# One tile turned by TensorE, sign bits folded into ten weight chunks, three engines' shares moved, and a new written order

## The chip, the cores and the metric

The kernel runs on one core of one Trainium2 chip. The metric is the time of one execution on the device, in microseconds (us); the time before is a median of 3 runs. TensorE does the matmuls (PE in the profile, PEld its weight loads), VectorE (DVE), ScalarE (ACT) and GpSimd (POOL) work beside it, and SyncE (SP) issues nearly all transfers (DMA).

## What is computed

Three layers follow each other, all results in float32: linear attention over 8 batches of 576 tokens with 8 heads of 64, a dense layer with a softmax-weighted activation and a layer norm, and a mixture of 8 experts of which each token takes one.

```python
# attention, per batch and head
q_s = softmax(q, axis=-1);  k_s = softmax(k, axis=2)
x = q_s @ (k_s.T @ v)                      # -> 4608 tokens x 512
# dense layer: w_in 512x1024, w_out 1024x512, both float64 in memory
h = x @ w_in
solu = h * softmax(h)
x2 = (layernorm(solu) * g_ln) @ w_out
# experts: w1 8x512x1024, w2 8x1024x512
logits = x2 @ w_gate + modality_bias[modality_id];  e = argmax(logits)
out = gate * (relu(x2 @ w1[e]) @ w2[e])
```

## The kernel before

A number that is multiplied is held as two float16 halves, `hi` and `lo`, and a product is three matmuls. So every operand passes a pair of steps: `hi_part` (ScalarE, a copy with a scale) and `lo_part` (the difference, on VectorE or GpSimd). Scales are powers of two, found from a maximum over all partitions: `diagonals` writes 128x128 diagonal matrices, a matmul with ones spreads them, and VectorE reduces.

The head of the program prepares weights. `w_in` and `w_out` come as float64 in 8 chunks of 128x512 each, and `to_f32` makes float32 of each by integer work. ScalarE makes the scaled high word (`p`, in PSUM), GpSimd makes 13 low bits (`x`), and VectorE joins them in two passes (the low bits, L618, then the sign, L620). One chunk of sixteen, number 14, is *folded*: its sign bits are put beside its low bits first, and VectorE needs one pass (L615). Chunks 0 to 7 are w_in, 8 to 15 are w_out in the order of rows `WO`.

Then the tokens pass in 36 tiles of 128. For tile t: `xT_mm` makes attention's output, `h_mm` (two halves of 12 matmuls) multiplies by w_in, `ln_unit` makes exp, norm and the halves `zhl` (ScalarE `za`, then VectorE `zl`, L1022), a DMA transpose turns `zhl` into `lnT` (`tr`, L1026), and `x2_mm` (48 matmuls, L1087) multiplies by w_out. `kv_mm` comes once a batch (60 matmuls, L869). `w_col` (96 small matmuls, L719) multiplies the turned w_out (`w_out_tr`, DMA transposes, L686) by the gate's weights once, and `w_col_split` puts the result beside w_out, so the first `x2_mm` needs it. After the tiles come 18 slots of 256 routed tokens (`slot_mm`, L1531 and L1552), each with 4 MB of expert weights, and a short tail.

Each step is a generator: `at(time, step)` files it, and every `yield` starts its next part. The string `ORDER` names all parts, some 2,900, in the order in which they are written into the program: an engine's own instructions run in that order, and an engine that waits holds up what is written behind it on the same engine. SP's transfers are in the same order. Tiles of PSUM named `big` (`ph`, `px`, `pcv`) share three buffers.

Of the kernel before, what the change touches and what calls it, by code (L numbers as in the profile page):

```python
# [73 lines left out]
w_col:7#0.0 zl:#0.0 ex:#10.0 w_col:6#0.0 v_split:1,3#0.1 tr:#35.0 w_col:3#0.0 v_split:1,1#0.0 v_split:1,2#0.1
w_col:5#0.0 ex:#10.1 v_split:1,4#0.1 ex:#39.0 w_col:2#0.0 lo:#10.0 mx:#12.0 w_col:4#0.0 zz:#1.1 tt:#2.0 h_mm:3,1#0.0
mx:#38.1 k_load:2,0#0.0 ex:#42.0 tr:#10.0 v_split:1,0#0.1 w_col_split:#0.0 ex:#40.0 fc:#0.1 ex:#38.0 w_col_split:#0.1
v_split:1,1#0.1 sq:#2.0 x2_mm:0#0.0 zl:#1.0 fc:#0.2 tr:#37.0 mx:#12.1 sc:#2.0 ex:#12.0 fc:#0.3 su:#4.0 zz:#2.0
su:#6.0 v_load:2#0.0 ex:#12.1 mx:#41.0 zz:#2.1 su:#4.1 kv_mm:1#0.0 mx:#11.0 ex:#41.0 zl:#2.0 fs:#0.0 hi:#36.0 hi:#4.0
tt:#3.0 tr:#39.0 lo:#36.0 kv_evac:1#0.0 sq:#3.0 x2_mm:1#0.0 lo:#12.0 tr:#38.0 sc:#3.0 kv_evac:1#0.1 su:#6.1 su:#5.0
v_sum:2,0#0.0 q_load:7#0.0 hi:#6.0 k_load:2,3#0.0 lo:#68.0 su:#5.1 zz:#3.0 kv_evac:1#0.2 hi:#5.0 v_sum:2,3#0.0  # L80
lo:#37.0 mx:#44.0 v_sum:2,4#0.0 xT_mm:4#0.0 lo:#38.0 tr:#40.0 x2_mm:2#0.0 xT_evac:4#0.0 mx:#44.1 hi:#37.0
q_load:9#0.0 v_sum:2,1#0.0 q_load:8#0.0 lo:#69.0 mx:#11.1 zz:#3.1 route:#0.0 xT_evac:4#0.1 route:#0.1 ex:#11.0
zl:#3.0 ex:#44.0 fc:#1.0 fc:#1.1 route:#0.2 mx:#14.0 su:#7.0 route:#0.3 h_mm:4,0#0.0 route:#0.4 v_sum:2,2#0.0
# [1776 lines left out]
```

## Time and profile before

| | us |
|---|---|
| median of 3 runs (lowest to highest) | 930.58 (930.48 to 931.44) |
| the profiled execution, own time | 932.11 |
| its span, from first to last record | 930.4 |
| PE busy (share of the span) | 847.3 (91%) |
| DVE busy | 776.5 (83%) |
| ACT busy | 700.5 (75%) |
| POOL busy | 520.4 (56%) |

The profiled execution lasted 1.5 us longer than the median, and 1.7 us of it lie outside the span. A busy PE is not a PE at its peak: a matmul's record covers its way through the array. PE's clock is full nearly everywhere; the granted clock falls below it at 50 to 60 us and 80 to 100 us, in one stretch at 380 to 400 us, and at the end.

### The profile page before, as it was taken

What the parts mean: (1) busy time and instruction counts of PE and PEld (TensorE: products, weight loads), DVE (VectorE), ACT (ScalarE), POOL (GpSimd) and SP (SyncE); (2) the same over time, 40 slices, a digit from 0 to 9 for tenths busy, and PEclk for the clock granted to TensorE, in tenths of its full rate; (3) what the DMA queues carried; (4) which work ended last, traced back from release to release, by engine and by line L of the source; (5) the groups of instructions that cost most, each with busy time, mean ns of one, the idle gap of its engine ahead of it and who ended that gap; (6) DMA issues with size and microseconds to landing.
All of it is one profiled execution on the core that took longest, in us unless ns stands there. A gap on an engine that the chain in (4) does not pass through costs nothing.

```text
span 930.4 us, 18754 instructions
## 1 busy us (share of the span) xinstructions
PE 847.3 (91%) x6565; PEld 585.7 (63%) x6565; DVE 776.5 (83%) x1589; ACT 700.5 (75%) x1041; POOL 520.4 (56%) x886
## 2 busy tenths in 40 slices
PE   0387999999998989898999999999999999999992
PEld 0264866686675766667667766756666666666671
DVE  6999789988987878788988699998889888888850
ACT  5658687977785887675687498877888888887851
POOL 7553787887888786754456765132234444434410
PEclk9988999999999999999999999999999999999997
DMA  8989899798699877678778988899999899999910
GB/s 322 293 177 231 179 191 207 163 225 186 134 203 194 175 166 153 159 102 212 176 185 230 277 259 241 263 279 320 303 301 275 273 286 286 270 288 272 273 66 12
DMA packets 275770, 204.83 MB, mean 220 GB/s; under 512 B 217617, under 2 KB 220241, under 8 KB 275666
## 3 DMA queue, kind: packets, MB, share of 16 engines
q1 hardware_dynamic: 268226, 183.51, 77.8%
q0 software_dynamic: 7152, 20.01, 6.4%
q8 instruction: 53, 0.87, 0.4%
q14 instruction: 51, 0.42, 0.1%
q10 hardware_dynamic: 288, 0.02, 0.0%
HBM read 130.94 MB, written 19.86 MB: 162 GB/s over the span
## 4 chain that ended last, share of the span: by engine, by line
PE 27%; DVE 27%; issue 12%; POOL 11%; ACT 10%; DMA 8%; SPq 2%; POOLq 0%; ACTq 0%; DVEq 0%
PE spo L1552 9%; PE sph L1531 8%; PE px L1087 6%; PE ph L968 3%; DVE t L998 3%; DVE hmx L986 2%; DMA out_dram<-kt,six 2%; DVE zhl L1022 2%; DMA six<-perm_scr 2%; DVE w1b L499 2%; ACT w1b L492 2%; DVE vhl L499 1%; POOL out_dram L1480 1%; ACT w2b L492 1%; DVE smm L1378 1%
## 5 line engine op out<-in xcount | busy, mean ns | idle before, releaser
L1087 PE MATMUL px<-w2b,lnT 128*128 128x256 f16 x1728 | 198.8, 276 | 4.0 <-DMA lnT<-zhl 4.0
L968 PE MATMUL ph<-w1b,xTt 128*128 128x512 f16 x864 | 198.3, 383 | 3.5 <-DVE rlg L1109 2.6
L1531 PE MATMUL sph<-vhl,w1b 128*128 128x256 f16 x1728 | 192.2, 273 | 1.9 <-DMA vhl<-kTt 1.7
L1552 PE MATMUL spo<-w2b,hh 128*128 128x512 f16 x864 | 191.1, 379 | 2.2 <-DVE hh L1544 2.2
L1087 PEld LDWEIGHTS <-lnT 128*128 128x128 f16 x1728 | 168.9, 98 | 32.5 <-DMA lnT<-zhl 5.8
L1531 PEld LDWEIGHTS <-w1b 128*128 128x128 f16 x1728 | 168.8, 98 | 26.7 <-DMA vhl<-kTt 2.5
L1466 POOL DMA_INDIRECT kTt<-xs_scr,six x38 | 53.7, 1413 | 173.5 <-DMA six<-perm_scr 127.5
L1552 PEld LDWEIGHTS <-hh 128*128 128x128 f16 x864 | 83.8, 98 | 100.9 <-DVE hh L1544 4.5
L968 PEld LDWEIGHTS <-xTt 128*128 128x128 f16 x864 | 82.9, 99 | 95.4 <-issue 6.1
L1480 POOL DMA_INDIRECT out_dram<-kt,six x37 | 48.0, 1298 | 51.3 <-ACT kt L1564 35.2
L992 ACT ACTIVATE e<-ph,hnm,ghb 128x1024 f32<-128x1024 f32 x32 | 38.3, 1197 | 27.7 <-DVE hnm L988 21.0
L1564 ACT ACTIVATE kt<-spo,srs 128x512 f32<-128x512 f32 x36 | 23.1, 682 | 47.8 <-issue 43.1
L499 DVE SCALAR_TENSOR_TENSOR w1b<-raw,sc,w1b 128x1024 f16<-128x1024 f32 x40 | 49.5, 1278 | 10.5 <-ACT w1b L492 10.4
L1016 ACT ACTIVATE e<-t,hna,ha 128x1024 f32<-128x1024 f32 x36 | 44.5, 1236 | 17.1 <-DVE hna L1013 11.9
L900 POOL TENSOR_TENSOR qr<-qr,qmx 128x512 f32<-128x512 f32 x36 | 40.3, 1121 | 23.9 <-DVE hmb L1007 14.4
L1022 DVE TENSOR_TENSOR zhl<-e,zhl 128x1024 f16<-128x1024 f32 x36 | 47.2, 1312 | 6.8 <-ACT zhl L1019 6.6
L1003 ACT ACTIVATE e<-t,hts 128x1024 f32<-128x1024 f32 x36 | 41.2, 1144 | 12.8 <-DVE t L998 11.8
L499 DVE SCALAR_TENSOR_TENSOR w2b<-raw,sc,w2b 128x1024 f16<-128x1024 f32 x40 | 49.9, 1275 | 0.9 <-ACT w2b L492 0.9
L1165 POOL DMA_INDIRECT perm_scr<-ids,rposi x36 | 39.9, 1109 | 16.0 <-POOL rposi L1163 6.5
L1378 DVE TENSOR_REDUCE smm<-raw 128x1 f32<-128x1024 f32 x40 | 47.7, 1208 | 1.0 <-DMA raw<-in_moe_w_dram 1.0
L921 POOL TENSOR_TENSOR qhl<-qr,qhl 128x512 f16<-128x512 f32 x36 | 42.6, 1187 | 10.5 <-ACT qhl L917 10.1
L869 PE MATMUL pk<-vhl,kTt 128*128 128x128 f16 x480 | 31.7, 230 | 16.0 <-DVE vhl L499 9.3
(284 smaller groups left out, 1732.7 us busy)
## 6 DMA issues: line engine op xcount, KB each, us to landing
raw<-in_moe_w_dram SPq DMA_DIRECT2D x88, 512.0 KB
qr<-in_q_dram SPq DMA_DIRECT2D x36, 256.0 KB
...
```

Of the source, the lines that this page charges most:

```text
L499: return e.scalar_tensor_tensor(out=lo, in0=src, scalar=scale, in1=hi, op0=ALU.mult, op1=ALU.subtract)
L921: G.tensor_tensor(out=g["hl"][:, 1], in0=qf, in1=g["hl"][:, 0], op=ALU.subtract)
L968: x = T.matmul(ph[:, n, :], xt[:, a, c, :], w1s[:, b2, c, n * 512:(n + 1) * 512], start=(c == 0 and (a, b2) == (0, 0)), stop=(c == 3 and a ...
L1003: mark["qa", t] = A.activation(out=g["e"], in_=g["t"], func=AF.Square, bias=g["mean"], scale=-1024.0, accum_out=var)
L1016: A.activation(out=g["e"], in_=g["t"], func=AF.Identity, bias=g["na"], scale=g["a"])
L1022: mark["zv", t] = V.tensor_tensor(out=g["z"][:, 1], in0=g["e"], in1=g["z"][:, 0], op=ALU.subtract)
L1087: T.matmul(px[:, n, 0:c1 - c0], lt[:, a, f, :], w2s[:, b2, f, c0:c1], start=(f == 0 and (a, b2) == (0, 0)), stop=(f == 7 and a == 1))
L1378: V.tensor_reduce(out=g["mm"][:, c:c + 1], in_=raws(i, 1, c), axis=AX.X, op=ALU.max, apply_absolute_value=True)
L1466: G.indirect_dma_start(out=gr[h], out_offset=None, in_=xs, in_offset=bass.IndirectOffsetOnAxis(ap=ix[:, h:h + 1], axis=0))
L1480: x = G.indirect_dma_start(out=out, out_offset=bass.IndirectOffsetOnAxis(ap=ix, axis=0), in_=ob, in_offset=None, bounds_check=NTOK - 1, oo ...
L1531: T.matmul(ph[:, ff, :], s1[:, a, c, f * 128:(f + 1) * 128], xt[:, 4 * b2 + c, :], start=(n == 0), stop=(n == 11))
L1552: T.matmul(po[:, h, :], hh[:, a, f, h * 128:(h + 1) * 128], s2[:, b2, f, 0:DM], start=(f == 0 and (a, b2) == (0, 0)), stop=(f == 7 and a = ...
```

## The change

Six things change.

1. Ten chunks are folded instead of one (`FOLD`): 0, 4, 6, 7 of w_in, 8, 9, 10, 13, 14, 15 of w_out. The sign is now a float16 zero with its sign bit, which ScalarE makes from the high word or GpSimd from its upper 16 bits.
2. `either` looks into a list of parts, `ON_POOL`. A part in it goes to another engine than by default. For the sign and the low bits the default is GpSimd and the other is ScalarE (six signs, five low parts). For the diagonals the default is VectorE and the other is ScalarE (five steps, six matrices: w_in, w_out, w_gate with two, v of batches 0 and 1). For three subtractions (`kv_evac` of batch 0, `w_out_split` 0 and 6) the other is GpSimd.
3. Tile 0 (`NTURN = 1`) has no DMA transpose: `turn` multiplies eight blocks of 128x128 of each half by an identity `eyeh` into a `big` tile, and ScalarE copies it to `lnT`.
4. `to_f32` has one more `yield`, so sign, low bits and joining can be placed apart.
5. The table of biases is made later (its two loads stood third and fourth on SP).
6. `ORDER` is written anew throughout.

```diff
-FOLD = (14,)
+FOLD = (0, 4, 6, 7, 8, 9, 10, 13, 14, 15)
+ON_POOL = """
+kv_evac:0#0.2 turn:0#0.1 turn:1#0.1 v_scale:0#0.1 v_scale:1#0.1 w_gate_split:#0.1 w_in_chunk:0,0#0.1
...
+    def either(e=G):
+        return e if here[0] in POOLED else V
...
         for i in range(n):
-            x = V.tensor_scalar(out=dg[:, i, :], in0=eye, scalar1=t[:, i:i + 1], scalar2=None, op0=ALU.mult)
-        return dg[:, 0:n, :], x
+            if either(A) is A:
+                A.activation(out=dg[:, i, :], in_=eye, func=AF.Copy, scale=t[:, i:i + 1])
+            else:
+                V.tensor_scalar(out=dg[:, i, :], in0=eye, scalar1=t[:, i:i + 1], scalar2=None, op0=ALU.mult)
+        return dg[:, 0:n, :]
...
-        G.tensor_scalar(out=xh[:, :, 0] if fold else x, in0=half[:, :, 1], scalar1=2.0 ** -13, scalar2=2.0 ** -14 - 0.5, op0=ALU.mult,
-                        op1=ALU.add)
         if fold:
-            G.tensor_scalar(out=xh[:, :, 1].bitcast(BF16), in0=hi.bitcast(F32), scalar1=0.0, scalar2=None, op0=ALU.mult)
-            yield
+            sign = xh[:, :, 1].bitcast(F16)
+            if either(A) is A:
+                A.activation(out=sign, in_=hi.bitcast(F32), func=AF.Copy, scale=2.0 ** -112)
+            else:
+                G.tensor_scalar(out=sign, in0=half[:, :, 3], scalar1=-2.0 ** -60, scalar2=32767.5 * 2.0 ** -60,
+                                op0=ALU.mult, op1=ALU.add)
+        yield
+        low = xh[:, :, 0] if fold else x
+        if either(A) is A:
+            A.activation(out=low, in_=half[:, :, 1], func=AF.Copy, scale=2.0 ** -13, bias=2.0 ** -14 - 0.5)
+        else:
+            G.tensor_scalar(out=low, in0=half[:, :, 1], scalar1=2.0 ** -13, scalar2=2.0 ** -14 - 0.5, op0=ALU.mult,
+                            op1=ALU.add)
+        yield
...
-        mark["kvv", b] = V.tensor_tensor(out=kvt[:, 1], in0=kvf, in1=kvt[:, 0], op=ALU.subtract)
+        mark["kvv", b] = either().tensor_tensor(out=kvt[:, 1], in0=kvf, in1=kvt[:, 0], op=ALU.subtract)
...
+        def turn(a):
+
+            if a == 0:
+                lnT[t] = ap2.tile([128, 2, 8, 128], F16, tag="lnT", name="lnT")
+            pt = psb.tile([128, 8, 128], F32, tag="big", name="pzT")
+            z = g["z"].rearrange("p a b s -> p a (b s)")
+            for f in range(8):
+                T.matmul(pt[:, f, :], z[:, a, f * 128:(f + 1) * 128], eyeh, start=True, stop=True)
+            yield
+            if either(A) is A:
+                A.activation(out=lnT[t][:, a], in_=pt, func=AF.Copy)
+            else:
+                V.tensor_copy(out=lnT[t][:, a], in_=pt)
...
-        at(time + 7.8, tr)
+        if t < NTURN:
+            at(time + 7.8, turn, 0)
+            at(time + 7.8, turn, 1)
+        else:
+            at(time + 7.8, tr)
```

On VectorE, between the scale of v (`cv`) and the first subtraction of v's halves (`vhl`), which `kv_mm` of batch 0 waits for, stood this before (`w1b` is w_in's halves, `raw` a chunk of w_out, `knmx` and `mg` small maxima):

```order
L477 TENSOR_SCALAR cv<-p2h 128x1
...
L443 TENSOR_SCALAR dg<-eye,p2b 128x128 x2
L499 SCALAR_TENSOR_TENSOR w1b_92<-e,csc,w1b_92 128x1024
L783 TENSOR_REDUCE knmx<-kt 128x1
L618 SCALAR_TENSOR_TENSOR pcv<-pcv,w2b_93 128x512
L620 SCALAR_TENSOR_TENSOR raw_95<-zhl,pcv 128x512
...
L499 SCALAR_TENSOR_TENSOR w1b_92<-t,csc,w1b_92 128x1024
L499 SCALAR_TENSOR_TENSOR vhl<-raw_96,cv,vhl 128x512 x5
```

and this after (line numbers are those of the changed kernel):

```order
L499 TENSOR_SCALAR cv<-p2h 128x1
L501 TENSOR_SCALAR icv<-p2h 128x1
L650 SCALAR_TENSOR_TENSOR raw_96<-pcv,w2b_94 128x512
L932 TENSOR_REDUCE qmx<-qr 128x8
L650 SCALAR_TENSOR_TENSOR raw_96<-pcv,w2b_94 128x512 x2
L521 SCALAR_TENSOR_TENSOR vhl<-raw_97,cv,vhl 128x512 x5
```

Two w_in subtractions and the diagonals have moved out from between, and three folded chunks with one pass each stand where two chunks with two passes stood.

On PE, in the changed kernel, the turn stands among the first `w_col` (`pg`) and the fourth tile's `h_mm`, ahead of the first `x2_mm` (weight loads and repeats are left out):

```order
L753 MATMUL pg<-wgs,w2b_94 128x8
...
L1065 MATMUL pzT<-eyeh,zhl 128x128
...
L753 MATMUL pg<-wgs,w2b_94 128x8
...
L1002 MATMUL ph<-w1b_93,xTt 128x512
...
L753 MATMUL pg<-wgs,w2b_94 128x8
...
L1002 MATMUL ph<-w1b_93,xTt 128x512
...
L1139 MATMUL px<-w2b_95,lnT 128x256
```

Before, all 96 of `pg` stood in one piece ahead of the last 12 `ph`; now they stand in four pieces of 24, the 16 `pzT` follow the second, and a piece of `ph` follows the third and the fourth.

On ScalarE, in the changed kernel, around the turn:

```order
L1050 ACTIVATE e<-t,hna,ha 128x1024
L1053 ACTIVATE zhl<-e 128x1024
L514 ACTIVATE vhl<-raw_97,cv 128x512 x2
L826 ACTIVATE kt,ksum<-kt,knmb 128x576
L1068 ACTIVATE lnT<-pzT 128x1024
L1026 ACTIVATE e,hes<-ph,hnm,ghb 128x1024
L1068 ACTIVATE lnT<-pzT 128x1024
```

The two copies of the turned halves are new, with the third tile's exp between them.

## Rows read from the trace of the kernel before

**Rows 1.** The page's 40 slices of 23.3 us: busy tenths, and the granted clock.
```profile
PE   0387999999998989898999999999999999999992
DVE  6999789988987878788988699998889888888850
PEclk9988999999999999999999999999999999999997
```

**Rows 2.** Busy time by stretch: length, PE, PEld, DVE, ACT, POOL, clock, DMA share, GB/s.
```profile
8.00:26.10 18.10, 3.53 (x28) 2.74 (x28) 17.23 (x33) 11.90 (x23) 14.92 (x18) 1.00 1.03 385
26.10:55.00 28.90, 11.41 (x101) 9.94 (x101) 27.82 (x62) 17.11 (x27) 17.74 (x19) 0.99 1.01 271
65.60:82.90 17.30, 16.00 (x136) 8.63 (x133) 16.95 (x38) 15.55 (x26) 1.88 (x3) 1.00 0.99 200
0.00:82.90 82.90, 41.12 (x329) 28.13 (x329) 72.74 (x156) 52.89 (x94) 44.65 (x67) 0.96 0.94 259
800.00:900.00 100.00, 100.00 (x698) 68.00 (x696) 85.02 (x102) 84.54 (x100) 39.00 (x26) 1.00 0.82 244
```

**Rows 3.** The chain that ended last, 60 to 120 us: start, length, what.
```profile
83.60 1.13 DVE zhl L1022
85.00 7.78 DMA lnT<-zhl
92.82 5.49 PE px L1087 x48
```

**Rows 4.** PE in order of time: start, length, in brackets the idle time before.
```profile
75.07 5.34 PE L968 MATMUL ph<-w1b,xTt 128*128 128x512 f16 x24
85.63 1.42 PE L719 MATMUL pg<-wgs,w2b 128*128 128x8 f16 x48 [4.04 <-DMA w2b<-w1b]
86.92 5.18 PE L968 MATMUL ph<-w1b,xTt 128*128 128x512 f16 x12
107.52 5.48 PE L1087 MATMUL px<-w2b,lnT 128*128 128x256 f16 x48
```

**Rows 5.** VectorE's groups, 0 to 93 us: count, busy us, mean ns.
```profile
L618 DVE SCALAR_TENSOR_TENSOR pcv<-pcv,w2b 128x512 int32<-128x512 int32 x15 | 10.4, 695 | 0.5
L499 DVE SCALAR_TENSOR_TENSOR w1b<-raw,gc,w1b 128x512 f16<-128x512 f32 x8 | 5.6, 746 | 0.0
L443 DVE TENSOR_SCALAR dg<-eye,p2b 128x128 bf16<-128x128 bf16 x6 | 3.4, 584 | 0.2
L886 DVE TENSOR_TENSOR kvs<-raw,kvs 128x512 f16<-128x512 f32 x1 | 0.7, 682 | 0.0
```

**Rows 6.** ScalarE's groups, 0 to 93 us.
```profile
L606 ACT ACTIVATE pcv<-w1b 128x512 f32<-128x512 f32 x12 | 7.4, 622 | 3.1 <-DVE e L620 2.2 <-DMA w1b<-in_moe_w_out_dram 0.5 <-DMA w1b<-in_moe_w_in_dram 0.2
L1019 ACT ACTIVATE zhl<-e 128x1024 f16<-128x1024 f32 x2 | 2.1, 1051 | 0.0
L492 ACT ACTIVATE wgs<-wgr,cg 128x32 f16<-128x32 f32 x1 | 0.3, 305 | 0.0
```

**Rows 7.** GpSimd's groups, 0 to 93 us.
```profile
L921 POOL TENSOR_TENSOR qhl<-qr,qhl 128x512 f16<-128x512 f32 x4 | 4.6, 1156 | 1.0 <-ACT qhl L917 0.9
L610 POOL TENSOR_SCALAR w2b<-w1b 128x512 int32<-128x512 uint16 x11 | 7.2, 650 | 3.4 <-DVE pcv L618 2.6
L613 POOL TENSOR_SCALAR w2b<-w1b 128x512 bf16<-128x512 f32 x1 | 1.7, 1683 | 0.1
```

**Rows 8.** VectorE and GpSimd in order of time, around 34 us and 43 us.
```profile
33.73 1.29 POOL L798 TENSOR_TENSOR khl<-w2b,khl 128x576 f16<-128x576 f32 x1
33.92 2.27 DVE L443 TENSOR_SCALAR dg<-eye,p2b 128x128 bf16<-128x128 bf16 x2
34.98 1.15 POOL L921 TENSOR_TENSOR qhl<-qr,qhl 128x512 f16<-128x512 f32 x1
...
42.66 3.39 DVE L499 SCALAR_TENSOR_TENSOR vhl<-raw,cv,vhl 128x512 f16<-128x512 f32 x5
```

**Rows 9.** SP's queue in order of time.
```profile
77.60 5.72 SPq L686 DMA_TRANSPOSE w2b<-w1b  x2
```

**Rows 10.** PE's `kv_mm` of batch 0 in order of time.
```profile
45.45 5.71 PE L869 MATMUL pk<-vhl,kTt 128*128 128x128 f16 x53 [0.85 <-DVE vhl L499]
```

More of the change, by code (lines that the diff above doesn't have):

```diff
@@ L74 @@
[L74 to L83, printed above, removed]
@@ L194 @@
-gate:#12.1 tt:#29.0 gate:#12.2 tr:#91.0 pick:2#0.0 sq:#29.0 one:2,1#0.0 v_split:7,0#0.1 idx:#1.0 fc:#13.2 one:2,0#0.0
-pick:3#0.0 kv_mm:7#0.0 fc:#13.3 hi:#63.0 hi:#62.0 sc:#29.0 kv_evac:7#0.0 zz:#29.0 x2_mm:28#0.0 zz:#29.1 fs:#13.0
-gather:1#0.0 kv_evac:7#0.1 hi:#34.0 gather:0#0.0 kv_evac:7#0.2 l1:0#0.0 fc:#14.0 lo:#95.0 one:2,3#0.0 one:1,0#0.0
-lo:#94.0 tr:#94.0 zl:#29.0 mx:1#0.0 h_mm:30,0#0.0 route:#13.0 pick:4#0.0 route:#13.1 lo:#65.0 xT_mm:31#0.0
-route:#13.2 mx:#100.0 route:#13.3 h_mm:30,1#0.0 xT_evac:31#0.0 tr:#96.0 route:#13.4 l1:3#0.0 xT_evac:31#0.1
@@ new lines @@
+lo:#11.0 rank:#0.1 ex:#43.0 v_scale:2#0.3 mx:#14.0 tr:#11.0 hi:#38.0 xT_mm:6#0.0 tt:#4.0 hi:#9.0 h_mm:5,1#0.0
+xT_evac:6#0.0 lo:#41.0 hi:#7.0 xT_evac:6#0.1 sq:#4.0 lo:#39.0 sc:#4.0 x2_mm:3#0.0 fs:#1.0 tr:#43.0 mx:#45.0 zz:#4.0
+mx:#14.1 rank:#0.2 q_load:12#0.0 su:#8.0 zz:#4.1 k_load:2,2#0.0 q_load:10#0.0 ex:#14.0 zl:#4.0 su:#8.1 ex:#45.0
+lo:#70.0 tr:#42.0 ex:#14.1 tt:#5.0 h_mm:6,0#0.0 hi:#8.0 lo:#14.0 hi:#39.0 mx:#54.0 v_split:2,1#0.0 mx:#13.0
+k_load:3,1#0.0 mx:#54.1 sq:#5.0 tr:#14.0 lo:#71.0 lo:#40.0 xT_mm:7#0.0 v_split:2,4#0.0 sc:#5.0 h_mm:6,1#0.0
@@ new lines @@
+ex:#19.0 tr:#55.0 kv_mm:3#0.0 kv_evac:3#0.0 mx:#20.1 fc:#4.3 ex:#20.0 ex:#66.0 tr:#57.0 sq:#11.0 ex:#19.1
+x2_mm:10#0.0 hi:#44.0 lo:#19.0 mx:#62.0 ex:#20.1 sc:#11.0 kv_evac:3#0.1 hi:#45.0 fs:#4.0 kv_evac:3#0.2 zz:#11.0
+gh_of:3#0.0 mx:#62.1 lo:#20.0 lo:#76.0 ex:#62.0 hi:#17.0 su:#18.0 v_sum:4,0#0.0 xT_mm:13#0.0 lo:#49.0 k_load:4,3#0.0
+v_sum:4,4#0.0 zz:#11.1 q_load:20#0.0 h_mm:12,0#0.0 fc:#5.0 fc:#5.1 lo:#77.0 k_load:4,2#0.0 xT_evac:13#0.0 tr:#59.0
+route:#4.0 su:#16.0 v_sum:4,1#0.0 route:#4.1 v_sum:4,3#0.0 xT_evac:13#0.1 v_sum:4,2#0.0 tr:#19.0 route:#4.2 zl:#11.0
@@ new lines @@
+zl:#22.0 xT_evac:25#0.0 tt:#23.0 tr:#78.0 h_mm:24,0#0.0 ex:#32.1 lo:#32.0 xT_evac:25#0.1 sq:#23.0 lo:#60.0
+k_load:7,3#0.0 hi:#57.0 sc:#23.0 xT_mm:26#0.0 tr:#83.0 v_split:6,3#0.0 v_split:6,1#0.1 h_mm:24,1#0.0 zz:#23.0
+fc:#11.0 mx:#94.0 tr:#85.0 xT_evac:26#0.0 mx:#90.0 mx:#94.1 zz:#23.1 lo:#89.0 q_load:31#0.0 fc:#11.1 x2_mm:22#0.0
+ex:#94.0 route:#10.0 zl:#23.0 mx:#34.0 tr:#80.0 mx:#90.1 fc:#11.2 route:#10.1 route:#10.2 mx:#83.0 route:#10.3
+fc:#11.3 v_split:6,3#0.1 ex:#83.0 h_mm:25,0#0.0 su:#32.0 route:#10.4 ex:#90.0 tt:#24.0 gate:#10.0 sq:#24.0
@@ new lines @@
+ex:#91.0 h_mm:29,1#0.0 route:#12.1 v_split:7,0#0.0 tr:#88.0 tt:#28.0 v_split:7,3#0.0 fc:#13.1 pick:0#0.0 sq:#28.0
+x2_mm:26#0.0 v_split:7,3#0.1 slot_buffers:#0.0 idx:#0.0 mx:#100.0 regs:#0.0 one:1,1#0.0 route:#12.2 sc:#28.0
+route:#12.3 one:1,2#0.0 route:#12.4 zz:#28.0 gate:#12.0 fc:#13.2 gate:#12.1 mx:#93.0 gate:#12.2 fc:#13.3 zz:#28.1
+tr:#91.0 ex:#93.0 zl:#28.0 x2_mm:27#0.0 tt:#29.0 pick:1#0.0 tr:#90.0 sq:#29.0 fs:#13.0 xT_evac:30#0.0 v_split:7,0#0.1
+one:2,2#0.0 pick:2#0.0 one:2,0#0.0 idx:#1.0 kv_mm:7#0.0 hi:#63.0 one:2,1#0.0 pick:3#0.0 sc:#29.0 x2_mm:28#0.0
@@ new lines @@
+route:#14.4 sp1:3#0.0 tr:#96.0 h_mm:33,1#0.0 fc:#15.1 xT_evac:34#0.0 sp1:3#0.1 sq:#32.0 gate:#14.0 one:1,3#1.0
+sp2:3#0.0 x2_mm:30#0.0 <lambda>:#19.0 sc:#32.0 gate:#14.1 gate:#14.2 sp1:2#0.1 idx:#3.0 zz:#32.0 tr:0#0.0 fc:#15.2
+sp2:0#0.0 sp2:3#0.1 fc:#15.3 sp2:2#0.0 mx:#101.0 sp2:1#0.0 xT_evac:34#0.1 sp1:1#0.0 rank:#12.1 xT_mm:35#0.0 sp2:1#0.1
+tr:1#0.0 x2_mm:31#0.0 xT_evac:35#0.0 ex:#101.0 xT_evac:35#0.1 one:2,3#1.0 sp2:0#0.1 fs:#15.0 regs:#2.0 zz:#32.1
+tt:#33.0 one:2,0#1.0 hi:#66.0 rank:#12.2 one:1,2#1.0 sp1:0#0.0 one:2,1#1.0 lo:#98.0 sp1:0#0.1 h_mm:35,0#0.0 hi:#67.0
@@ L360, in tile_attn_moe_moe @@
     strict = [True]
+    here = [""]
+    def either(e=G):
+        return e if here[0] in POOLED else V
     def when(name, part, time):
@@ L410, in flush @@
             time, n, base, name, part, marks, fn, args = queue.pop(0)
+            here[0] = f"{name}.{part}"
             if strict[0] and time > STRICT:
```

570 lines of the change are left out of this document (288 added, 282 removed).

## The prediction

> **What bounds the kernel now.** I read the slices first, then stretches, then the chain, then the groups of the head of the program. In the slices PE is at 8 or 9 tenths from the fifth on, and at 0, 3, 8 and 7 in the first four [rows 1]; late in the program it is busy throughout at the full clock [rows 2]. So from about 93 us on PE sets the pace, and time can be won where PE stands still: ahead of the first `x2_mm`. There VectorE is the full engine: 17.2 of 18.1 us, 27.8 of 28.9 and 16.95 of 17.3 in the three stretches [rows 2]. ScalarE has air in the first two (11.9 and 17.1) and hardly any in the last (15.55 of 17.3). The transfers fill their engines through 55 us (share 1.03, then 1.01). The chain says the same: it comes down VectorE to tile 0's `zhl`, ending at 83.60 + 1.13 = 84.7, passes the DMA transpose (7.78), and from 92.82 it is PE's [rows 3].
>
> What PE does before 92.8 it need not do later, so idle PE is not all lost. The order of PE's large pieces ahead of the first `x2_mm` holds as much work after as before (four tiles' `h_mm` and `xT_mm`, one `kv_mm`, the 96 `pg`) plus the turn. I therefore take the shift of the first `x2_mm` as the gain.
>
> **The change, part by part.** *Folding.* VectorE's first pass goes from 15 chunks to 6: 9 x 0.695 = 6.3 us [rows 5], four of them (2.8) in w_in's stretch, five (3.5) in w_out's. *Diagonals.* Six matrices leave VectorE: 3.4. *Subtractions.* `kvs` of batch 0 is 0.7, two of w_out's eight are 2 x 0.746 = 1.5 [rows 5]. Together 11.9 us less work on VectorE ahead of tile 0's `zhl`. Rows that only move behind it (one `hmx`, one `xTt`) I leave out, since they come later.
>
> Who takes it over: ScalarE gets 11 passes like its strided reads of the same chunks (0.622 each, 6.8 us) and six matrices (a pass of 32 columns takes 0.305 [rows 6]; six are 1.8, and at the other end, at 0.622, 3.7). GpSimd loses five low parts (5 x 0.65 = 3.3), and gets four signs, of which the nearest rows are 0.65 (16-bit input) and 1.68 (the old sign) [rows 7]: 2.6 to 6.7. It also gets three subtractions at 1.16 and two scalings at about 0.65, 4.8 in all.
>
> How much of VectorE's 11.9 comes through, by stretch:
> - w_in (8 to 26 us): GpSimd was busy 14.9 of 18.1 [rows 2]. It now makes six low parts instead of eight (-1.3) and two signs (1.3 to 3.4), so it does not get shorter, and the loads are at a share of 1.03. Of 2.8 us I take 0.9; the ends are -2.1 (GpSimd sets it with the slow sign) and 2.8.
> - w_out and batch 0's `kv_mm` (26 to 66 us): 3.5 + 3.4 + 0.7 = 7.6. Here the order matters too: the first five `vhl` subtractions, which ran at 42.66 [rows 8], now stand behind three folded chunks instead of two w_in subtractions, two full chunks and the diagonals. ScalarE was busy 17.1 of 28.9 [rows 2] and gets most of its new passes here (about 5.6): covered. I take 7.0; the ends are 3.5, if the DMA share of 1.01 holds back the last loads of w_out, and 7.6.
> - the first tiles (66 to 83 us): 1.5. ScalarE has 1.7 us of air; without that cover, nothing comes through. I take 1.0.
>
> Sum 8.9: tile 0's `zhl` at 75.8 instead of 84.7.
>
> *The turn.* Before, 8.1 us passed from `zhl` to `x2_mm`. After it, PE does eight `pzT` of the second half (at 5.71/53 = 0.108 as in `kv_mm` [rows 10]: 0.9), ScalarE's copy of it takes 1.05 as `zhl` does [rows 6] beside 24 `pg` (half of 1.42 [rows 4]), then come 12 `ph` (half of 5.34, 2.67), 24 `pg` (0.7) and 12 `ph` (2.67): 0.9 + 1.05 + 2.67 + 0.7 + 2.67 = 8.0. The turn itself wins next to nothing over the transpose: PE had this work anyway. What goes is the standstill in it: 4.04 on the turned w_out, and the 12 `ph` that ran at half the clock after it (5.18 against 2.67 [rows 4]). The fourth tile's `ph` needs the copy, since `big` tiles are three; behind the turn, the whole of PE waits for `zhl`. PE's work ahead of the old wait ended at 81.6 (85.63 - 4.04); shifted by as much as `zhl` it ends at about 72.7 now, and the turn's second half waits for 75.8. That is nearly as long a wait as the old one, so the low clock may come back: 2.5 us or nothing. I take the middle, 1.25. The turned w_out is not late: its last transposes took 5.72 to issue from 77.60 [rows 9], behind a subtraction that now comes some 7 us sooner.
>
> So the first `x2_mm` starts at 75.8 + 8.0 + 1.25 = 85.05 against 92.82: 7.8 us sooner. Tiles 1 and 2 keep their DMA transposes; tile 2's `x2_mm` began at 107.52 without a wait [rows 4] and is asked for at 99.7, its `zhl` being as much sooner: no more lost. Later waits I take as equal; the new order can move them by some us either way. The profiled execution's 932.1 becomes 924.3, and the median, 1.5 below it, 930.6 - 7.8 = **922.8 us**.
>
> **A shared port.** VectorE's two diagonals of one pair took 2.27 us and ended at 33.92 + 2.27 = 36.19, while GpSimd ran two passes back to back that ended at 34.98 + 1.15 = 36.13 [rows 8]; the mean of all six is 0.58 for 128 columns. The Trainium skill ("SBUF — State Buffer", section "Who interferes with whom") says that VectorE and GpSimd share a pair of ports under an exclusive lock, and that a VectorE instruction with two SBUF inputs waits for a GpSimd instruction that reads SBUF. By that rule the trace agrees for the diagonals, and moving three subtractions to GpSimd is a cost to VectorE as well as a relief; no row here separates it. In rows: GpSimd's new 4.8 us would hold VectorE's other subtractions up as the pair was held. That is the fourth rival.
>
> **Rivals.**
> - *All of VectorE's work comes through* (11.9; PE's clock stays full): 930.6 - 11.9 = 918.7. For it: VectorE is full in all three stretches. Against it: ScalarE's last stretch, the loads.
> - *The head is set by loads and GpSimd*: only the lower end in the middle and 0 in w_in: 3.5: 927.1. For it: the DMA shares above 1.
> - *The lead is given back*: `lnT` of tile 1 or 2, or a later stage, comes at the old time; 930.6. Against it: 100 of 100 us busy later [rows 2].
> - *GpSimd's passes hold VectorE up*: 4.8 of 7.8 lost: 927.6.
> - *Slower: ScalarE takes the bound.* By 82.9 it was busy 52.9 [rows 2] and idle 30.0. If those 30.0 are waits that stay, its new 6.8 + 1.8 come on top, and tile 0's `zhl` is 8.6 later than before: 939.2. It decides as soon as the idle time hides less than all of the 8.6, since then ScalarE and no longer VectorE releases `zhl`. Against it: ScalarE waited there for VectorE and GpSimd [rows 6], whose work gets less.
>
> **How the numbers follow.** Forecast (7.8, own range 919.5 to 925.5): 0.46. All of it: 0.18. Loads and GpSimd: 0.14. Port: 0.06. Given back: 0.06. ScalarE: 0.10. Faster by over 0.2% (1.9 us, about what a measurement can tell from no change): 0.84; same 0.06; slower 0.10. The range reaches from under the second case, by 2 us for a better order later, to over the third and fourth: 916.5 to 929.
>
> **What would show it.** Right: VectorE's `vhl` subtractions of batch 0 some 7 us sooner than 42.66; tile 0's `zhl` at 74 to 78; `pzT` at once behind it; the first `px` at 82 to 87; the same distance from there to the end. Wrong: ScalarE without idle time from 26 us on; VectorE waiting for GpSimd's signs in w_in; PE waiting for `lnT` of tiles 1 or 2 by more than a us; a longer way from the first `px` to the end, which would mean that the written order, not the head, makes the time.

## The result and the profile after

The changed kernel took 941.49 us (median of 3, 938.95 to 943.7) against 930.58: 1.0113 times as long, interval 1.0071 to 1.0155. The profiled execution lasted 943.7, its span 941.7.

The page's slices, as in [rows 1]: busy tenths and granted clock.

```profile
PE   1498999979999999898999979979999999999993
PEclk9788999999999999999999999989999999999997
```

TensorE starts sooner, as forecast, and has new dips at about 190 to 210, 540 to 565 and 610 to 635 us. The stretches of [rows 2], in the same columns, and then two later ones:

```profile
8.00:26.10 18.10, 5.88 (x48) 4.70 (x48) 16.04 (x31) 13.27 (x26) 15.75 (x28) 1.00 1.09 370
26.10:55.00 28.90, 14.27 (x130) 12.06 (x129) 25.47 (x57) 24.78 (x44) 18.32 (x19) 0.65 1.03 268
65.60:82.90 17.30, 12.36 (x131) 7.23 (x131) 16.95 (x35) 14.79 (x24) 10.98 (x14) 0.84 1.05 243
...
157.00:240.00 83.00, 76.95 (x642) 53.57 (x640) 67.68 (x171) 65.10 (x121) 63.32 (x131) 0.98 0.86 170
...
540.00:640.00 100.00, 88.32 (x582) 57.17 (x581) 83.19 (x148) 75.01 (x94) 41.98 (x46) 0.95 0.89 242
```

The last two of the kernel before:

```profile
157.00:240.00 83.00, 81.12 (x704) 57.29 (x703) 72.24 (x187) 68.25 (x123) 67.37 (x136) 1.00 0.88 190
...
540.00:640.00 100.00, 94.43 (x670) 64.51 (x668) 93.39 (x169) 85.05 (x106) 37.50 (x43) 1.00 0.92 265
```

In the head VectorE is no longer full in the second stretch (25.5 of 28.9) and ScalarE does 24.8 there instead of 17.1. TensorE's granted clock is 0.65 there, before it was 0.99; TensorE is busy for half of that stretch or less in both kernels. Later, in the 183 us of the last two rows, TensorE is busy 10.3 us less than before, and that is work put off, since it has the same matmuls to do.

TensorE in order of time, from the turn to the third `x2_mm`, then its three longest waits (start, length, idle time before in brackets):

```profile
75.22 0.62 PE L1065 MATMUL pzT<-eyeh,zhl 128*128 128x128 f16 x8 [1.82 <-ACT zhl L1053]
78.05 1.03 PE L1065 MATMUL pzT<-eyeh,zhl 128*128 128x128 f16 x8 [2.20 <-DVE zhl L1056]
80.19 4.71 PE L1002 MATMUL ph<-w1b,xTt 128*128 128x512 f16 x12 [0.49 <-ACT lnT L1068]
87.93 5.48 PE L1139 MATMUL px<-w2b,lnT 128*128 128x256 f16 x48
103.27 5.49 PE L1139 MATMUL px<-w2b,lnT 128*128 128x256 f16 x48 [0.49 <-DMA lnT<-zhl]
...
207.48 6.94 PE L1139 MATMUL px<-w2b,lnT 128*128 128x256 f16 x48 [4.20 <-DMA lnT<-zhl]
...
559.18 0.17 PE L1202 MATMUL pr<-cum,ones 128*128 128x8 f16 x1 [4.63 <-POOL cum L1213]
...
617.70 0.37 PE L1450 MATMUL pm<-dg,oneb 128*128 128x256 bf16 x1 [4.84 <-DVE dg L464]
```

Against [rows 3, 4]: tile 0's `zhl` ends at 78.0 instead of 84.7, the first `px` starts at 87.93 instead of 92.82. From there to the end of the span it is 941.7 - 87.9 = 853.8 us, before 930.4 - 92.8 = 837.6: 4.9 won ahead of the first `px`, 16.2 lost behind it. The kernel before has no wait above 2.6 us behind 93 us. The changed one has these three, and behind them matmuls at a lower granted clock (0.78 from 207.5 to 214.4 us, 0.79 from 559.2 to 565.9, 0.50 from 617.7 to 623.0).

**Where the wait at 559 comes from.** SyncE's queue in the changed kernel (`six` are slot 2's token numbers, 1 KB; `xs_scr` are the last tiles' rows on their way to memory; `raw` are weights, 512 KB each). The three gathers further down (`kTt`) fetch a slot's rows from `xs_scr`; `cum` adds up the tokens of each expert, and TensorE's `pr` reads it:

```profile
535.90 0.33 SPq L1412 DMA_DIRECT2D raw<-in_moe_w_dram  x1
541.79 0.38 SPq L1510 DMA_DIRECT2D six<-perm_scr  x1
542.42 0.38 SPq L1415 DMA_DIRECT2D raw<-in_moe_w_dram  x1
543.01 0.34 SPq L1412 DMA_DIRECT2D raw<-in_moe_w_dram  x1
543.61 0.37 SPq L1415 DMA_DIRECT2D raw<-in_moe_w_dram  x1
544.09 0.89 SPq L1195 DMA_DIRECT2D xs_scr<-xrows  x2
```

What the DMA engines did from 535 to 560 us, in 40 slices of 0.6 us (busy tenths):

```profile
DMA  0799999792002289989745999999996186176899
```

And GpSimd in the same time:

```profile
553.54 1.01 POOL L1518 DMA_INDIRECT kTt<-xs_scr,six  x1 [7.79 <-DMA xs_scr<-xrows]
554.86 1.44 POOL L1518 DMA_INDIRECT kTt<-xs_scr,six  x1 [0.30 <-issue]
556.60 2.01 POOL L1518 DMA_INDIRECT kTt<-xs_scr,six  x1 [0.30 <-issue]
558.64 0.48 POOL L1213 TENSOR_TENSOR cum<-cum,roh 128x8 f16<-128x8 f16 x2
```

The queue stands for 5.6 us ahead of `six`, and the DMA engines run empty at about 541 to 543 us. Then three weight loads are issued in 1.2 us, the rows come behind them, and the gathers wait for the rows until 553.5. `cum` stands behind three gathers on GpSimd, and `pr` waits for `cum`. Before, `six` for slot 2 was issued at 477.52. SyncE's store of the rows and the first gather from them, in the kernel before:

```profile
543.22 1.02 SPq L1143 DMA_DIRECT2D xs_scr<-xrows  x2
546.85 1.01 POOL L1466 DMA_INDIRECT kTt<-xs_scr,six  x1 [2.98 <-DMA xs_scr<-xrows]
```

### The profile page after: what moved, and what is told of

Read it like the earlier page. It is cut to its first block, busy times and chain, and to the rows that moved or that the text cites. A ratio compares the mean times of both kernels' runs of the same rounds, so it can differ in the third digit from the quotient of the medians.

```text
span 941.7 us, 18754 instructions
## 1 busy us (share of the span) xinstructions
PE 853.4 (91%) x6581; PEld 587.5 (62%) x6581; DVE 775.5 (82%) x1571; ACT 709.2 (75%) x1060; POOL 511.4 (54%) x890
## 4 chain that ended last, share of the span: by engine, by line
PE 27%; DVE 24%; POOL 13%; issue 12%; ACT 10%; DMA 9%; SPq 2%; POOLq 0%; ACTq 0%; DVEq 0%
PE spo L1604 11%; PE sph L1583 9%; PE ph L1002 3%; PE px L1139 3%; DVE t L1032 3%; DMA out_dram<-kt,six 2%; DVE hmx L1020 2%; DVE zhl L1056 2%; DMA raw<-in_moe_w_dram 2%; DVE smm L1430 2%; DMA lnT<-zhl 2%; ACT w1b L514 1%; DMA xs_scr<-xrows 1%; DVE vhl L521 1%; POOL perm_scr L1217 1%
## 5 line engine op out<-in xcount | busy, mean ns | idle before, releaser
L1604 PE MATMUL spo<-w2b,hh 128*128 128x512 f16 x864 | 195.1, 385 | 1.6 <-DVE hh L1596 1.1
L1518 POOL DMA_INDIRECT kTt<-xs_scr,six x38 | 48.4, 1274 | 146.0 <-DMA six<-perm_scr 90.6
L1532 POOL DMA_INDIRECT out_dram<-kt,six x37 | 56.1, 1516 | 85.6 <-ACT kt L1616 70.8
L1050 ACT ACTIVATE e<-t,hna,ha 128x1024 f32<-128x1024 f32 x36 | 44.5, 1236 | 25.0 <-DVE hna L1047 23.3
L514 ACT ACTIVATE w1b<-raw,sc 128x1024 f16<-128x1024 f32 x40 | 43.9, 1140 | 11.6 <-DVE sc L488 11.6
L1596 DVE TENSOR_TENSOR hh<-rl,hh 128x1024 f16<-128x1024 f32 x36 | 43.9, 1219 | 8.2 <-ACT hh L1594 8.0
```

Of the source, the lines that this page charges most:

```text
L514: return A.activation(out=hi, in_=src, func=AF.Copy, scale=scale)
L1050: A.activation(out=g["e"], in_=g["t"], func=AF.Identity, bias=g["na"], scale=g["a"])
L1518: G.indirect_dma_start(out=gr[h], out_offset=None, in_=xs, in_offset=bass.IndirectOffsetOnAxis(ap=ix[:, h:h + 1], axis=0))
L1532: x = G.indirect_dma_start(out=out, out_offset=bass.IndirectOffsetOnAxis(ap=ix, axis=0), in_=ob, in_offset=None, bounds_check=NTOK - 1, oo ...
L1604: T.matmul(po[:, h, :], hh[:, a, f, h * 128:(h + 1) * 128], s2[:, b2, f, 0:DM], start=(f == 0 and (a, b2) == (0, 0)), stop=(f == 7 and a = ...
```

## The experiments

Times are medians of 5 to 12 executions. Ratios, with 95% intervals, are to the kernel before, timed beside each group: e1 to e4 (its median 930.0), e5 to e8 (931.0), e9 to e12 (930.9), f1 to f4 (931.9), g1 and g2 (931.4). A ratio is not the quotient of the two medians: for e11 that would be 1.0026 instead of 1.0001. One kernel's executions lay 2.5 to 13 us apart, so a difference under some 2 us between two rows is not told.

| run | what it is | us | ratio |
|---|---|---|---|
| e1 | new to tile 2, old behind | 932.3 | 1.0038 [1.0020, 1.0056] |
| e2 | new to tile 29, old behind | 935.5 | 1.0061 [1.0040, 1.0083] |
| e3 | old to tile 2, new behind | 942.8 | 1.0155 [1.0126, 1.0185] |
| e4 | old to tile 29, new behind | 939.9 | 1.0106 [1.0090, 1.0122] |
| e5 | changed, slot 2's numbers early | 933.2 | 1.0025 [1.0004, 1.0047] |
| e6 | before, slot 2's numbers late | 931.6 | 1.0007 [0.9983, 1.0030] |
| e7 | before, 15 passes left out (weights lose their signs) | 922.9 | 0.9915 [0.9884, 0.9946] |
| e8 | before, 7 passes twice | 936.7 | 1.0060 [1.0033, 1.0087] |
| e9 | new to tile 6, old behind | 931.6 | 0.9997 [0.9967, 1.0027] |
| e10 | e9 without the turn | 927.9 | 0.9960 [0.9929, 0.9990] |
| e11 | e5, one load early too | 933.3 | 1.0001 [0.9971, 1.0032] |
| e12 | e5, tiles 6 to 12 in old order | 934.9 | 1.0035 [1.0001, 1.0068] |
| f1 | folding alone, old order | 928.7 | 0.9972 [0.9949, 0.9996] |
| f2 | moves alone, old order | 932.8 | 1.0009 [0.9982, 1.0037] |
| f3 | folding and moves, old order | 931.8 | 0.9999 [0.9979, 1.0019] |
| f4 | e11 without the turn | 932.9 | 1.0016 [0.9996, 1.0036] |
| g1 | e10 without the moves | 927.6 | 0.9950 [0.9929, 0.9972] |
| g2 | e10, subtractions back | 930.8 | 0.9981 [0.9954, 1.0007] |

### Where the new order loses (e1 to e4)

The two orders are joined at an `x2_mm`: the names up to it from one, the rest in the order of the other. In effect, for e1:

```diff
-TIMES = {name: i for i, name in enumerate(ORDER.split())}
+NEW, OLD = ORDER.split(), ORDER_BEFORE.split()
+head = NEW[:NEW.index("x2_mm:2#0.0") + 1]
+TIMES = {name: i for i, name in enumerate(head + [x for x in OLD if x not in head])}
```

**e1.** 

> The changed kernel, with its own order up to the third tile's x2_mm; everything behind it stands in the old order. Theory A (the new order of the tiles and of the passage to the experts loses what the head wins): the lead of 4.9 us at the first px stays, 930.6 - 4.9 = 925.7, between 924 and 928, and the waits of 4.2 at 207 us, 4.6 at 559 and 4.8 at 618 are gone. Theory B (the lead itself makes the later waits, since transfers and loads stay where they were): the waits come back with the old order, 935 to 942. Theory C (something that the new head leaves behind, such as the late table of biases or ScalarE's and GpSimd's backlog, slows the tiles): also 935 to 942, but with waits in the first ten tiles.

**e2** joins at `x2_mm:29`. 

> The changed kernel, with its own order up to the x2_mm of tile 29, and the old order from there: the last tiles, the passage to the experts and the slots. Theory A: the head's 4.9 are lost again in the tiles (PE is level with before at 388 us), the passage costs no more than before: 930.6, between 928 and 933. Theory B or C: 938 to 942, as the changed kernel.

**e3** is the kernel before with NEW and OLD exchanged. 

> The kernel before, with its own order up to the third tile's x2_mm; everything behind it stands in the new order. Theory A: the new order costs its 16 us without the head's lead: 930.6 + 16 = 946.6, between 940 and 949. Theory B and C: no new head, so no new waits: 929 to 933.

**e4** is e3 joined at `x2_mm:29`. 

> The kernel before, with the new order only from the x2_mm of tile 29 on. Theory A: the passage to the experts alone costs 10 to 11 us (the waits at 559 and 618 us, with the slow clock behind them): 941, between 937 and 943. Theory B and C: 929 to 933.

e3 and e4 came out as theory A says: without the new head, the new order of the passage to the experts costs 9.9 us and with the tiles' order 12.8. So the loss is not a consequence of the lead. e2 fell between the two ranges (5.5 us more than before): the passage's loss is gone, but what is left of the new order, with the joint, costs more than the head's lead. e1 missed theory A too: its first `px` came at 87.03, and it took 2.3 us more than before. TensorE waited 1.98 us at 115 us for `xTt`, which VectorE had to make right behind the joint; the joint is part of what e1 measures.

### One step moved (e5, e6, e11)

```diff
-idx:#3.0 zz:#32.0
+idx:#3.0 idx:#2.0 zz:#32.0
...
-sp2:0#1.1 idx:#2.0 sp2:3#1.0
+sp2:0#1.1 sp2:3#1.0
```

**e5.** 

> The changed kernel with one step moved: the transfer of slot 2's token numbers (six), a few KB, stands on SyncE's queue where it stood before, ahead of the last tiles' transfers, instead of among slot 3's weight loads. Theory A1 (this transfer waits for the last ranks' scatters to land and holds the queue up for 5.6 us; three weight loads of 512 KB are then issued at once ahead of the tokens' rows, the gathers wait for the rows, GpSimd's cum stands behind the gathers, and TensorE behind cum): the 4.6 us at 559 go, and the 4.8 at 618, which come from the table of slots being late, go with them: 941.5 - 10 = 931.5, between 929 and 935. Theory A2 (the two waits have causes of their own: the gather that now stands ahead of cum, and the place of the later weight loads): 936 to 939, with the wait at 618 left. Theory A3 (the order of the matmuls makes it): 940 to 943.

```profile
536.86 0.38 SPq L1412 DMA_DIRECT2D raw<-in_moe_w_dram  x1
537.51 0.47 SPq L1409 DMA_DIRECT2D raw<-in_moe_w_dram  x1
538.98 0.38 SPq L1412 DMA_DIRECT2D raw<-in_moe_w_dram  x1
542.48 1.01 SPq L1192 DMA_DIRECT2D xs_scr<-xrows  x2
...
547.84 1.02 POOL L1515 DMA_INDIRECT kTt<-xs_scr,six  x1 [2.23 <-DMA xs_scr<-xrows]
...
551.52 0.69 POOL L1210 TENSOR_TENSOR cum<-cum,roh 128x8 f16<-128x8 f16 x2
```

These rows of e5's queue and of GpSimd show the same three loads 5 us sooner, the gather at 547.84 and `cum` at 551.5 instead of 558.6. No wait of TensorE at 559 is left, and 1.0113 became 1.0025: 0.88% of 931 is 8.2 us by moving one transfer of 1 KB. With the intervals of the two ratios, that is an estimate good to about 4.4 us either way. Theory A1's time came, but only its first half is borne out: the wait at 618 did not go with the other, it stayed as 4.04 at 614.

**e6** moves the same name in the kernel before from its early place to behind `sp2:0#1.1`. 

> The kernel before with the same one step moved the other way, to the place that it has in the changed kernel. Theory A1: the queue is held up there too, 930 + 10 = 940, between 936 and 943. Theory A2: 932 to 936. Theory A3: 929 to 931.

It cost 0.6 us, nothing that can be told, as in theory A3 and against A1. There `six` went at 540.38 with two weight loads behind it instead of three, `cum` (551.51) stood behind two gathers instead of three, and TensorE had more matmuls ahead of `pr`. The late transfer alone is not enough; it needs what the new order puts around it.

**e11** moves `one:1,2#5.0` ahead of `idx:#5.0` besides. 

> The changed kernel with two steps moved: slot 2's token numbers as in the run that gave 933.2, and one weight load of slot 5 ahead of slot 5's token numbers, as before the change. Theory A2 (the second wait, 4.0 us for dg at 614 us, is that load held up on SyncE's queue by the token numbers of slot 5, which wait for the table of slots): 933.2 - 3.5 = 929.7, between 928 and 931.5. If another load or VectorE's order makes that wait: 932 to 934.5.

TensorE's waits in e11, 575 to 625 us:

```profile
580.51 0.27 PE L1447 MATMUL pm<-dg,oneb 128*128 128x256 bf16 x1 [0.63 <-DVE dg L461]
582.67 10.65 PE L1580 MATMUL sph<-vhl,w1b 128*128 128x256 f16 x96 [1.89 <-DMA vhl<-kTt]
599.62 5.40 PE L1580 MATMUL sph<-vhl,w1b 128*128 128x256 f16 x48 [3.70 <-DMA vhl<-kTt]
608.56 0.27 PE L1447 MATMUL pm<-dg,oneb 128*128 128x256 bf16 x1 [0.95 <-DVE dg L461]
```

The wait for `dg` fell from 4.04 to 0.95, so that load was its cause, and two waits for a slot's turned tokens (1.89 and 3.70) stand in its place. The time stayed the same (933.3 against 933.2; the ratios, 1.0001 and 1.0025, can't be told apart).

### Is the first px what counts (e7, e8)?

```diff
-        V.scalar_tensor_tensor(out=p.bitcast(I32), in0=p.bitcast(I32), scalar=3, in1=x, op0=ALU.logical_shift_left,
-                               op1=ALU.bitwise_or)
-        return V.scalar_tensor_tensor(out=dst.bitcast(I32), in0=hi, scalar=SIGN, in1=p.bitcast(I32),
-                                      op0=ALU.bitwise_and, op1=ALU.bitwise_or)
+        return V.scalar_tensor_tensor(out=dst.bitcast(I32), in0=p.bitcast(I32), scalar=3, in1=x,
+                                      op0=ALU.logical_shift_left, op1=ALU.bitwise_or)
```

**e7.** 

> The kernel before with VectorE's second pass over 15 chunks left out, so that w_in and w_out lose their signs: 15 x 0.695 = 10.4 us less of VectorE's work in the head, nothing else moved. The step of the prediction (what the first x2_mm wins, the end wins): the first px starts 6 to 10 us sooner and the time falls as much, 920 to 925. Theory D (between 93 and 390 us the chain of waits runs through VectorE, ScalarE and GpSimd, not TensorE, so a lead of TensorE is used up there): the first px 6 to 10 sooner and the time 929 to 931.

**e8** makes the second pass twice where n >= 8. 

> The kernel before with VectorE's second pass over w_out's seven chunks made twice: 7 x 0.695 = 4.9 us more in the head, the result the same. The step of the prediction: 930 + 4 to 5 = 934 to 935. Theory D: TensorE's delay is taken up by its slack in the tiles as far as VectorE's own delay allows: 930 to 932.

e7's first `px`, and the place of e8's is 96.72:

```profile
85.29 5.49 PE L1085 MATMUL px<-w2b,lnT 128*128 128x256 f16 x48 [1.34 <-DMA lnT<-zhl]
```

7.5 us sooner gave 8.1, 3.9 later cost 5.7. Theory D, that the tiles use a lead up, falls. Where nothing else changes, the head's shift is about what the end gets. One thing is not shown: with its signs gone, e7 may route tokens to other experts, and no run tells what that alone does to the time.

### Lead and tiles (e9, e12)

**e9** is e1 joined at `x2_mm:6`. 

> The changed kernel with its own order up to the seventh tile's x2_mm (157 us, where its lead on TensorE is still 4.9 us) and the old order behind it. Unlike the first experiment, where the orders were joined at the third tile and TensorE waited 2 us for xTt right behind the joint, the joint lies where both orders have written nearly the same steps. Theory E (the head's lead of 4.5 to 5 us lasts as long as the queue of SyncE lets it; the new order loses it at 190 to 210 us and loses 10 more at the passage): 930.6 - 4.5 = 926, between 924.5 and 928, faster than both kernels. Theory F (the new head leaves VectorE or the queues behind, so that any order gives the lead back): 930 to 933, as in the first experiment.

**e12** is e5 with the names between `x2_mm:6` and `x2_mm:12` sorted as before. 

> The changed kernel with slot 2's token numbers early (933.2) and the steps between the x2_mm of tiles 6 and 12 (157 to 241 us) in the old order among themselves. Theory E1 (three transposes of k and a store of the tokens' rows stand ahead of the third lnT there, and two transposes of q behind it; the waits of 1.0 and 4.2 us at 193 and 206 go): 933.2 - 4.5 = 928.7, between 927 and 930.5. If the lead is lost anyway by 388 us, where all kernels so far stand within 1.4 us: 932 to 934.5.

Neither gain came. e9's time lies in the range of theory F, e12's 0.4 above its second range. But e9's profiled execution, its fastest, kept the lead to the end (927.55), and e10 and g1 below, with the same order, are faster than the kernel before, so theory F's reason (any order gives the lead back) is not shown either. In e12 e5's wait of 4.15 at 206 became one of 1.65 at 201, and 3.38 came at the joint:

```profile
244.50 5.72 PE L1136 MATMUL px<-w2b,lnT 128*128 128x256 f16 x35 [3.38 <-DMA lnT<-zhl]
```

### The parts of the head (e10, f1 to f4, g1, g2)

```diff
-NTURN = 1
+NTURN = 0
```

**e10**, with `tr` where `turn:0#0.0` stood. 

> The kernel of the experiment before it, with tile 0 turned by the DMA transpose again, issued at the place where the turn's first half stood. By the prediction's step (the turn wins next to nothing over the transpose: 8.0 against 8.1 us, and 1.25 for the clock): the same time within 2 us, 925 to 928. If the turn is worth what the standstill of 4.0 and the slow 12 ph cost before: 4 to 6 us more, 930 to 932.

TensorE in e9 and, below it, e10, from the first `px`:

```profile
86.54 5.48 PE L1136 MATMUL px<-w2b,lnT 128*128 128x256 f16 x48
95.21 5.48 PE L1136 MATMUL px<-w2b,lnT 128*128 128x256 f16 x48
```

```profile
83.69 0.49 PE L1135 MATMUL px<-w2b,lnT 128*128 128x256 f16 x3
...
94.16 5.49 PE L1135 MATMUL px<-w2b,lnT 128*128 128x256 f16 x48 [1.10 <-DMA lnT<-zhl]
```

Without the turn the first `px` is 2.9 us sooner, the second 1.05, and the time 3.7 lower (3.1 by the means, give or take 1.8). The prediction's step had them equal, so it fell.

The next three are the changed code with the old order (each new part behind the one that it was split from) and `NTURN = 0`. **f1** has the signs and low bits of `ON_POOL` alone, **f2** `FOLD = (14,)` and the rest of `ON_POOL`, **f3** both.

```diff
-FOLD = (0, 4, 6, 7, 8, 9, 10, 13, 14, 15)
+FOLD = (14,)
...
+kv_evac:0#0.2 v_scale:0#0.1 v_scale:1#0.1 w_gate_split:#0.1 w_in_scale:#0.1 w_out_scale:#0.1 w_out_split:0#0.1
+w_out_split:6#0.1
```

**f1.** 

> The kernel before, in its old order, with one part of the change alone: ten chunks are folded, their signs and low bits made on ScalarE or GpSimd as in the change. If VectorE's nine passes (6.3 us) come through as the prediction has them (0.9 in w_in's stretch, 3.5 in w_out's): 931 - 4.4 = 926.6, between 924.5 and 928. If ScalarE's and GpSimd's new passes take the lead back: 929 to 932.

**f2.** 

> The kernel before, in its old order, with the other part alone: six diagonals go from VectorE to ScalarE and three subtractions to GpSimd. If VectorE's 5.6 us come through: 931 - 4 to 5 = 926 to 927. If they lie beside waits, or GpSimd's two passes of each moved subtraction are late for who needs them: 929 to 932.

**f3.** 

> Both parts together in the old order, tile 0 turned by the DMA transpose: the change without its new order and without the turn. If VectorE's 11.9 us come through as in the run that left 10.4 out and gave 922.9: 922 to 925, the fastest so far. If the new order of the head is needed for it: 926 to 931.

**f4** is e11 with `NTURN = 0`. 

> The changed kernel with the two steps moved that gave 933.3, and tile 0 turned by the DMA transpose. If the turn costs the 3 to 4 us that it cost with the old order behind it: 929.5 to 931. If that was the old order's own doing: 932 to 935.

Its time is within 0.5 us of e11's: with the new order behind it, what the turn costs at the first `px` (83.54 in f4) does not reach the end.

Tile 0's `zhl` in the kernel before, f1, f2 and f3, in this order:

```profile
83.50 1.22 DVE L1022 TENSOR_TENSOR zhl<-e,zhl 128x1024 f16<-128x1024 f32 x1
```

```profile
79.29 1.22 DVE L1049 TENSOR_TENSOR zhl<-e,zhl 128x1024 f16<-128x1024 f32 x1
```

```profile
82.45 1.22 DVE L1049 TENSOR_TENSOR zhl<-e,zhl 128x1024 f16<-128x1024 f32 x1
```

```profile
80.20 1.22 DVE L1049 TENSOR_TENSOR zhl<-e,zhl 128x1024 f16<-128x1024 f32 x1
```

The folding brings it 4.2 forward, the moves 1.05, both 3.3. At the end, f1 is 3.3 lower, just outside its first range, f2 is not lower, and f3 gives 0.2: with the moves added to it, the folding's gain is gone (f3 against f1: 2.5 us more by the means, give or take 2.0). f2's VectorE and GpSimd, 0 to 93 us, in groups, and then the same subtractions in the changed kernel:

```profile
L514 DVE SCALAR_TENSOR_TENSOR w1b<-raw,gc,w1b 128x512 f16<-128x512 f32 x6 | 5.6, 968 | 1.7 <-ACT w1b L507 1.7
L514 DVE SCALAR_TENSOR_TENSOR w1b<-e,csc,w1b 128x1024 f16<-128x1024 f32 x2 | 3.6, 1790 | 0.0
```

```profile
L512 POOL TENSOR_SCALAR raw<-raw,gc 128x512 f32<-128x512 f32 x2 | 3.6, 1797 | 0.0
L513 POOL TENSOR_TENSOR w1b<-raw,w1b 128x512 f16<-128x512 f32 x2 | 2.6, 1312 | 0.2
```

```profile
L521 DVE SCALAR_TENSOR_TENSOR w1b<-raw,gc,w1b 128x512 f16<-128x512 f32 x6 | 4.2, 748 | 0.0
```

GpSimd took two of eight w_out subtractions. In f2 VectorE's other six take 5.6 us, as its eight did [rows 5], and VectorE waits 1.7 for ScalarE besides. In the changed kernel, where the order puts other steps beside GpSimd's passes, the six take 4.2 at the old 748 ns each. The two of 1790 are 2.31 and 1.27: the longer one ran at 33.19 us, beside two GpSimd passes (`khl`, `qhl`) that in the kernel before stand beside two diagonals, which took 2.27 [rows 8]. With the diagonals gone, the next instruction met the same passes.

**g1** and **g2** are e10 with parts of `ON_POOL` taken out: all but signs and low bits in g1, the three subtractions in g2.

**g1.** 

> The kernel with the new order to tile 6, the old order behind it and no turn (927.9), with diagonals and subtractions back on VectorE: of the change the folding and the head's order alone. If GpSimd's passes held VectorE up by as much as they took over: 926 to 928.5, as fast or faster; the diagonals' 3.4 us on VectorE against 2.1 on ScalarE count for up to 2 the other way. If the moves are worth their 5.6 us in this order: 931 to 933.

**g2.** 

> The same kernel with only the three subtractions back on VectorE; the diagonals stay on ScalarE. If GpSimd's passes held VectorE up: 925.5 to 927.5, the fastest result with correct weights. If the subtractions are worth their 2.2 us: 929.5 to 931.

g1, which has only the folding and the head's new order, is at 0.995 below both kernels. g2, timed beside it, takes 3.3 us more (3.0 by the means, give or take 1.9), and its interval takes in 1: with the subtractions back the gain did not return, so they alone do not eat it, and the diagonals on ScalarE win nothing here. Tile 0's `zhl` ends at 77.72 in g1 and 77.63 in e10: in the new order all the moves together bring it 0.1 us forward.

## Why the prediction was wrong

**The step that failed** is "Later waits I take as equal; the new order can move them by some us either way". From the first `px` to the end the way became 16.2 us longer. The kernel before lost 12.8 with the new order behind its third tile (e3) and 9.9 with the new order from tile 29 on (e4), and the place of a single transfer was worth 8.2 (e5). That it had moved stood in the order of the changed kernel, on SyncE: slot 2's token numbers were issued 64 us later, in the middle of slot 3's weights. The prediction looked at the order up to the first `x2_mm` only. Of its rivals "The lead is given back" comes nearest, but it ended at the old time; none has a loss behind the first `px`. "ScalarE takes the bound" gave nearly the time and was not the cause: ScalarE is busy 24.8 of 28.9 us in the fullest stretch, and tile 0's `zhl` came sooner, not later. The last of the signs that it named, a longer way from the first `px` to the end, is what happened.

**"I take the shift of the first x2_mm as the gain"** held where only the work in the head was changed: 7.5 for 8.1 (e7), -3.9 for -5.7 (e8), 3.3 for 3.3 (f1). It did not hold with the moves or the turn: 3.3 for 0.2 in f3, 6.3 for about nothing in e9. Why is open. From the first `px` to the end of the span, 837.6 us before, the profiled executions took 836.3 in f3 and 838.7 in e9, but 840.1 in f1 and 844.1 in g1, whose medians are lower; with one profile of each, this can't tell.

**The terms.**
- *Folding*: 4.4 us were taken (0.9 and 3.5); f1's `zhl` is 4.2 sooner and its time 3.3 lower (0.4 to 4.7 by its interval). Right in the sum.
- *Diagonals and subtractions*: 4.5 of 5.6 were taken (3.4, 0.7 and a part of 1.5); f2's `zhl` is 1.05 sooner, and in the new order the moves bring 0.1 (g1 against e10). This term was mis-sized. Of the 3.4 us of diagonals, 2.27 were one pair held up beside GpSimd [rows 8]: six diagonals on VectorE take 1.9 in g1. GpSimd's scaling pass, estimated at 0.65, takes 1.80 in f2 and 1.66 in the changed kernel, and in f2 VectorE's subtractions beside GpSimd's passes take 968 ns instead of 746. That was the fourth rival's mechanism. The Trainium skill ("SBUF — State Buffer", section "Who interferes with whom") has a VectorE instruction with two SBUF inputs contend with a GpSimd instruction that reads SBUF; by that rule f2's subtractions are held up, and its trace agrees (968 ns against 746). In the changed kernel VectorE's w_out subtractions are not held up (748 ns). Its five `vhl` subtractions took 4.30 us at 34.81, before 3.39 [rows 8], but beside GpSimd's passes for folded chunks: in g1, without the moves, they took 4.29. Why the moves bring so little in the new order is open.
- *The table of biases* was put at nothing. Made later, VectorE's `m` (before at 4.64 us) stands right ahead of tile 0's `zhl`, whose input ScalarE had ready at 75.17, and GpSimd's passes for the table run beside it:

```profile
74.11 1.06 ACT L1053 ACTIVATE zhl<-e 128x1024 f16<-128x1024 f32 x1
74.88 1.27 DVE L603 CAST m<-modi 128x36 f32<-128x36 int32 x1
76.28 1.71 DVE L1056 TENSOR_TENSOR zhl<-e,zhl 128x1024 f16<-128x1024 f32 x1
```

  So `zhl` starts 1.1 us late and takes 1.71 instead of 1.22: an estimate of 1.6 us from these rows, and no run moves the table back.
- *The turn*: 8.0 us and 1.25 for the clock were taken from `zhl` to `px`; it was 87.93 - 77.99 = 9.9. After waits of 1.82 and 2.20 us the granted clock fell to 0.50, the lower of its two levels (1.2 GHz), from 78.05 to 80.19 us, and was 0.56 while the 12 `ph` ran, in 4.71 instead of 2.67: the low clock came back, and the middle had only half of it. And the turn did not win "next to nothing". Without it (e10) the first `px` starts at 83.69, 6.1 us behind `zhl` at 77.63 and without a wait for `lnT`; the turn cost 2.9 us at the first `px`.
- *The sum*: `zhl` was forecast at 75.8 and ended at 78.0, 2.2 later, and the turn took 0.7 more. So 4.9 of the 7.8 us came at the first `px`: the folding's 4.2, and the new order of the head and the moves, less the table of biases and the turn.
- *Tiles 1 and 2* lost no more, as said: 0.49 at 103.27.

**What stays open.** Of the 16.2 us behind the first `px`, the one transfer explains about half. The rest is not traced to a cause. A part lies in the tiles' new order: e2 against e9 puts it at 0.6%, e3 against e4 at 0.5%, while e11, which has it too, stands level with e9. Putting the stretch of tiles 6 to 12 back did not win it (e12).
